# Conversion of the second layer's output weights begun at the end of the attention at a lower pace, and the seven-product block's sums taken from copies over three pairs

## The chip, the core and the metric

The kernel runs on one core of a Trainium2 chip. The engines that matter are TensorE (PE, with its weight loads PEld), VectorE (DVE), ScalarE (ACT) and the queue on which SyncE (SP) issues transfers. The metric is device microseconds of one execution; lower is better.

## The reference

Everything is float32. Attention for 4 batches, 8 heads, 576 positions and 64 columns per head, half of the heads with a local and half with a strided causal mask; its output, as a matrix x of 2304 tokens by 512, goes through two feed-forward layers of the same shape:

```python
h = np.maximum(x @ w_in, 0.0)       # 512 -> 2048
x = (h * h) @ w_out                 # 2048 -> 512, twice, with weights of their own
```

## The kernel before

**Precision.** The matrix engine takes each float32 operand as two parts, a high one (a ScalarE copy into `F32R`) and the rest (VectorE's difference). A product is three matmuls: high by high, high by rest, rest by high. So every operand costs one ScalarE copy and one VectorE subtraction.

**First layer.** Tokens go in blocks k = 0 to 4 of 512, except block 3 of 256. A step s is one slice of 128 hidden units (two slices in a block of 256). The loop runs `mm1(s + 1)` (24 matmuls of 256 columns, or 12 of 512), then `mm2(s)` (as many), and between groups of matmuls it calls `point()`, 8 times a step, where other work is put into the program. Blocks 0 to 2 are steps 0 to 47, block 3 is 48 to 55, block 4 is 56 to 71. `mm1` ends with ScalarE making `r`, `sq`, `gh` and VectorE making `gl`; `mm2` of that step needs `gh` first and `gl` last. At a block's end ScalarE copies four banks to `o` (tag `pt`, two buffers), and each `o` is stored to `y_dram`.

**Attention** fills points up to step 46 or 47.

**Conversion of the second layer's weights** (`conv2`). Its 32 pieces arrive as 64-bit words and are put together by shifts on VectorE and a scaling on ScalarE (`sign2`, `range2`, `whole2`), split (`high2`, `rest2`), and combined into four sums (`sums_1`, `sums_2`, `high_s`, `sums_3`). Pieces go in pairs, first 8 pairs of w_out, then 8 of w_in, 9 rows of the list `conv2` to a pair; a point adds `PACE` to a credit, and each whole credit puts one row into the program. A pair of w_out writes 1 MB of units into the first half of a staging area in `xall` (stored by L378 to `w_mem`) and 1 MB of sums into the second half (stored by L427). The area is single: `high2` of the next pair waits for the store by L378, `high_s` of the next for the store by L427. ScalarE runs in program order, so `r`, `sq` and `gh` of a step stand behind these copies.

**Second layer.** Block 5 (256 tokens; steps 72 to 79) is done by `narrow`, which reads units back (`narrow_w`, `ring_load`) and prepares the operands of the next block (`x_works`, `load_x`). Its last step and the four blocks after it use a scheme of seven products (`seven`, `frame`): per pair q of hidden slices one frame of 84 matmuls of 256 columns. A frame has four visits, which make hidden values in one bank `ps_m`: (11, s2), then (12), then (s1, s3), then (s4, 22); between them, as gaps of 9, 9, 15 and 9 matmuls, the products of the pair before, into seven banks. A visit writes over `ps_m`, so it waits for the additions by VectorE (L1080) that read the visit before. At a block's end the seven banks are summed (`first_sum`, `sums_late`, `sums_then`) and stored, while the next block's products begin to write over them. During a block the operands of the next are made from its `y_dram`, one of `x_works` per frame.

Of the kernel before, what the change touches and what calls it, by code (L numbers as in the profile page):

```python
# [17 lines left out]
P = 128  # L18
# [44 lines left out]
PACE, START_2 = 0.72, 4  # L63
# [106 lines left out]
def tile_attention_then_two_mlps(  # L170
# [263 lines left out]
    for i in range(0, half2 + 2, 2):  # L434
        old, new = i > 0, i < half2
        if new:
            conv2 += [[(sign2, i)], [(sign2, i + 1), (range2, i)]]
        conv2.append([(sums_3, i - 2)] * old + [(range2, i + 1)] * new)
        if new:
            conv2 += [  # L440
                [(whole2, i)],
# [583 lines left out]
    def mm2(s, point):  # L1025
# [28 lines left out]
        for m, (i, c, y, lhsT, rhs) in enumerate(todo):  # L1054
# [19 lines left out]

    def parts(hi, lo, src):
        nc.scalar.activation(out=hi, in_=src, func=AF.Copy)  # L1076
        tt(lo, src, r32(hi), ALU.subtract)
# [45 lines left out]

    def narrow(s, point):
# [4 lines left out]
        if q + 1 < NF // 2:  # L1129
            if q == 0:  # L1130
                load_x(NB + 1)
            else:
                for one in work[q - 1]:
                    one()
# [9 lines left out]
        for one in work[-1]:  # L1144
            one()
        todo = narrow_products(s)
        frame([todo[3 * i:3 * i + 3] for i in range(4)], (NB + 1, 0), None)
# [20 lines left out]
    def load_x(k):  # L1168
        t0, n = BLOCKS[1][k - NB]
        for c in range(KC):  # L1170
            nc.sync.dma_start(out=others[:, c * TB:(c + 1) * TB], in_=y_dram[:, c, t0:t0 + n])

    def x_works(k):
# [5 lines left out]
        def nothing():  # L1179
            pass  # L1180

        def op(i, src):
            return lambda: parts(*x_op(k, i), src)

        return [
            (nothing, op(0, b11)),
            (nothing, op(2, b21)),
            (lambda: tt(b11, b12, b11, ALU.subtract), op(3, b11)),
            (lambda: tt(b12, b22, b12, ALU.subtract), op(4, b12)),
            (lambda: tt(b11, b22, b11, ALU.subtract), op(1, b11)),  # L1190
            (lambda: tt(b21, b21, b11, ALU.subtract), nothing),
            (op(5, b22), op(6, b21)),
# [25 lines left out]
    def g_op(name):  # L1218
        tile, i = {
            "11": ("b", 0), "a22t4": ("b", 1), "s2t2": ("b", 2), "s4b22": ("b", 3),  # L1220
            "s1t1": ("a", 0), "s3t3": ("a", 1), "12": ("a", 2),
# [54 lines left out]
    def frame(gaps, nxt, cur, heads=(), copy=None, early=None, work=None, late=()):  # L1276

        k, q = nxt
        if not of:
# [6 lines left out]
            of["al"] = gpool.tile([P, 3 * HALF], F32R, tag="gl", name="al", bufs=2).rearrange(  # L1286
                "p (i n) -> p i n", i=3)
# [3 lines left out]
        heads = list(heads)  # L1291
        s24 = None
        if cur:
# [5 lines left out]
            nc.scalar.activation(out=ah[:, 2], in_=a12, func=AF.Copy)  # L1299
            if heads:  # L1300
                for one in heads[:2]:
                    one()
                tt(al[:, 2], a12, r32(ah[:, 2]), ALU.subtract)
                for one in heads[2:]:
                    one()
            tt(s13[:, 0], a21, a22, ALU.add)
            tt(s13[:, 1], a11, a21, ALU.subtract)
            if not heads:
                tt(al[:, 2], a12, r32(ah[:, 2]), ALU.subtract)
# [6 lines left out]
        u2, u3 = m[:, HT:], u[:, HT:]  # L1316
        u4 = u[:, :HT]
        nc.scalar.activation(out=m, in_=ps, func=AF.Copy, scale=W_BACK)  # L1318
        if cur:
            nc.scalar.activation(out=ah[:, 0:2], in_=s13, func=AF.Copy)  # L1320
            nc.scalar.activation(out=bh[:, 2:4], in_=s24, func=AF.Copy)
        tt(u2, m[:, :HT], m[:, HT:], ALU.add)
# [270 lines left out]
```

## Time and profile before

| what | value |
|---|---|
| median of 3 runs | 945.41 us (944.93 to 946.8) |
| the profiled execution | 947.56 us, of which the span from first to last instruction is 945.8 us |
| PE busy | 881.1 us, 93% |
| DVE busy | 685.6 us, 72% |
| ACT busy | 521.2 us, 55% |
| DMA | 155.21 MB, mean 164 GB/s |
| mean granted TensorE clock | 0.98 |

PE is busy nearly all the time, so what counts is where its stages take longer than their matmuls do. In time order: start and attention beside blocks 0 to 2 to about 364 us, blocks 3 and 4 to about 536, block 5 to about 589, the frames of seven products to 926, the last products and sums to 945.8.

### The profile page before, as it was taken

What the parts mean: (1) busy time and instruction counts of PE and PEld (TensorE: products, weight loads), DVE (VectorE), ACT (ScalarE), POOL (GpSimd) and SP (SyncE); (2) the same over time, 40 slices, a digit from 0 to 9 for tenths busy, and PEclk for the clock granted to TensorE, in tenths of its full rate; (3) what the DMA queues carried; (4) which work ended last, traced back from release to release, by engine and by line L of the source; (5) the groups of instructions that cost most, each with busy time, mean ns of one, the idle gap of its engine ahead of it and who ended that gap; (6) DMA issues with size and microseconds to landing.
All of it is one profiled execution on the core that took longest, in us unless ns stands there. A gap on an engine that the chain in (4) does not pass through costs nothing.

```text
span 945.8 us, 16062 instructions
## 1 busy us (share of the span) xinstructions
PE 881.1 (93%) x5719; PEld 784.4 (83%) x5719; DVE 685.6 (72%) x1745; ACT 521.2 (55%) x1201; POOL 17.7 (2%) x15
## 2 busy tenths in 40 slices
PE   8899999999999999979788779999989989998998
PEld 8788888888888889957566668999989989998998
DVE  5898973887767752766568766677877786777766
ACT  6887773676666553555456644544434444444442
POOL 0700000000000000000000000000000000000000
PEclk9999999999999999988989989999999999999999
DMA  8955512222221203487773285555575566555563
GB/s 271 342 181 169 188 42 75 66 84 73 87 92 59 61 11 116 154 298 286 265 256 100 85 295 195 178 168 169 184 227 172 178 202 209 170 172 185 187 189 124
DMA packets 81247, 155.21 MB, mean 164 GB/s; under 512 B 7440, under 2 KB 36240, under 8 KB 78096
## 3 DMA queue, kind: packets, MB, share of 16 engines
q1 hardware_dynamic: 81168, 154.19, 49.3%
q8 instruction: 45, 0.74, 0.3%
q14 instruction: 34, 0.28, 0.1%
HBM read 127.95 MB, written 26.21 MB: 163 GB/s over the span
## 4 chain that ended last, share of the span: by engine, by line
PE 58%; DVE 21%; ACT 11%; DMA 7%; issue 3%; SPq 0%; DVEq 0%; ACTq 0%
PE ps_h L969 15%; PE ps_y L969 14%; PE ps_m L1237 13%; PE ps_y L1264 7%; DMA w_mem<-xall 3%; DVE s L386 3%; DVE r L1080 2%; DVE bl L386 2%; PE ps_s L626 2%; DVE xall L386 2%; PE ps_x L702 2%; DVE gl L1022 2%; PE ps_pt L758 1%; ACT sq L1017 1%; ACT gh L1018 1%
## 5 line engine op out<-in xcount | busy, mean ns | idle before, releaser
L969 PE MATMUL ps_h<-xall,w 128*128 128x512 f32 (+1 forms) x1153 | 247.4, 358 | 0.0
L969 PEld LDWEIGHTS ps_h<-xall,w 128*128 128x128 f32 x1153 | 185.5, 189 | 26.2
L969 PE MATMUL ps_y<-gh,w 128*128 128x512 f32 (+1 forms) x640 | 162.8, 386 | 25.3 <-ACT gh L1018 18.8
L969 PEld LDWEIGHTS ps_y<-gh,w 128*128 128x128 f32 x640 | 109.7, 193 | 48.9 <-ACT gh L1018 24.5
L1237 PE MATMUL ps_m<-xall,s 128*128 128x256 f32 x768 | 113.5, 292 | 18.0 <-DVE r L1080 9.5
L1237 PEld LDWEIGHTS ps_m<-xall,s 128*128 128x128 f32 x768 | 99.3, 194 | 28.4 <-DVE r L1080 17.7
L1022 DVE TENSOR_TENSOR gl<-sq,gh 128x512 fp32r<-128x512 f32 x80 | 55.3, 691 | 61.8 <-ACT gh L1018 55.5
L1264 PE MATMUL ps_y<-w,bh 128*128 128x256 f32 x496 | 93.5, 281 | 0.0
L969 PE MATMUL ps_y<-gl,w 128*128 128x512 f32 (+1 forms) x324 | 85.8, 377 | 0.0
L1012 ACT ACTIVATE r<-ps_h 128x512 f32<-128x512 f32 x80 | 47.4, 592 | 65.8 <-PE ps_h L969 56.9
L1237 PE MATMUL ps_m<-xall,w 128*128 128x256 f32 x576 | 82.7, 279 | 0.0
L1264 PEld LDWEIGHTS ps_y<-w,bh 128*128 128x128 f32 x496 | 76.7, 190 | 0.0
L1237 PEld LDWEIGHTS ps_m<-xall,w 128*128 128x128 f32 x576 | 74.0, 188 | 0.4 <-ACT u L1318 0.4
L386 DVE TENSOR_TENSOR bl<-r,bh 128x256 fp32r<-128x256 f32 x64 | 27.2, 425 | 64.8 <-ACT bh L1076 37.1
L1264 PE MATMUL ps_y<-w,ah 128*128 128x256 f32 x372 | 70.9, 279 | 0.0
L1021 DVE TENSOR_TENSOR sq<-r 128x512 f32<-128x512 f32 x41 | 28.3, 691 | 58.2 <-ACT r L1012 58.2
L1264 PE MATMUL ps_y<-w,bl 128*128 128x256 f32 x248 | 69.4, 280 | 0.0
L969 PEld LDWEIGHTS ps_y<-gl,w 128*128 128x128 f32 x324 | 56.9, 192 | 10.8 <-DVE gl L1022 1.0
L1264 PEld LDWEIGHTS ps_y<-w,ah 128*128 128x128 f32 x372 | 57.0, 189 | 0.0
L1264 PE MATMUL ps_y<-w,al 128*128 128x256 f32 x186 | 52.6, 283 | 0.0
L674 ACT ACTIVATE s<-s,m 96x128 f32<-96x128 f32 (+2 forms) x88 | 34.3, 390 | 33.1 <-DVE m L558 32.5
L1299 ACT ACTIVATE ah<-c 128x256 fp32r<-128x256 f32 x31 | 13.0, 418 | 69.0 <-DVE c L1246 68.8
(121 smaller groups left out, 1510.5 us busy)
## 6 DMA issues: line engine op xcount, KB each, us to landing
w<-w_mem SPq DMA_DIRECT2D x221, 256.0 KB, 2.7
raw<-moe_w_in_d SPq DMA_DIRECT2D x32, 512.0 KB, 6.1
w_mem<-xall SPq DMA_DIRECT2D x16, 1024.0 KB, 5.2
raw<-moe_w_out_d SPq DMA_DIRECT2D x24, 512.0 KB, 5.0
xall<-w_mem SPq DMA_DIRECT2D x8, 1024.0 KB, 5.4
qk<-loc_qk_d SPq DMA_DIRECT2D x12, 416.0 KB, 3.0
out_d<-o SPq DMA_DIRECT2D x17, 256.0 KB, 3.9
y_dram<-o SPq DMA_DIRECT2D x16, 256.0 KB, 2.0
```

The lines of the kernel that those rows point to most:

```text
L386: nc.vector.tensor_tensor(out=out, in0=in0, in1=in1, op=op)
L626: nc.tensor.matmul(sv[:, h, g], lhsT=t[:, (h * ng + g) * nq:(h * ng + g + 1) * nq], rhs=t[:, 2 * ng * nq + g * ks:2 * ng * nq + g * ks + n ...
L674: nc.scalar.activation(out=blk, in_=blk, func=AF.Exp, scale=-1.0, bias=m[:nq, j:j + 1], accum_out=dens[i][:nq, j:j + 1],)
L702: nc.tensor.matmul(ps[:, 2 * g * nq:2 * (g + 1) * nq], lhsT=v[:nk, g * P:(g + 1) * P], rhs=pt[:, :, g], start=True, stop=True,)
L969: nc.tensor.matmul(y[:, c:c + w], lhsT=lhsT, rhs=rhs[:, c:c + w], start=start and c == 0, stop=stop and c + w == n,)
L1012: nc.scalar.activation(out=r, in_=ps, func=AF.Relu, scale=W_BACK)
L1021: nc.vector.tensor_tensor(out=sq, in0=r, in1=r, op=ALU.mult)
L1022: nc.vector.tensor_tensor(out=lo, in0=sq, in1=r32(h), op=ALU.subtract)
L1080: nc.vector.scalar_tensor_tensor(out=dst, in0=src, scalar=sign * W_BACK, in1=to, op0=ALU.mult, op1=ALU.add)
L1237: nc.tensor.matmul(ps[:, half * HT:(half + 1) * HT], lhsT=w[:, j * P:(j + 1) * P], rhs=x[:, j], start=half == 0 and j == 0 and m == 0, sto ...
L1264: nc.tensor.matmul(banks[name][:, t * HALF:(t + 1) * HALF], lhsT=g[:, rows], rhs=w, start=first and t == 0 and m == 0, stop=end and t == 1 ...
L1299: nc.scalar.activation(out=ah[:, 2], in_=a12, func=AF.Copy)
```

## The change

The conversion. It begins when the attention's last row has been put into the program, not at step 50; its first four loads are issued there too; the pace is 0.6 rows a point for w_out's pairs and 0.68 for w_in's, in place of 0.72. `sums_3` becomes a row of its own, and its store goes ahead of the load that used to precede it. The stores of `y_dram` of blocks 3 and 4 are issued by ScalarE.

The frames. VectorE's first addition after visit (12) goes ahead of the two subtractions (`al`, `bl` of 512 columns) that stood before it; the additions after visit (s1, s3) go ahead of the subtraction of `bh[0]` and of the next block's operand. Each of the next block's operands is subtracted for in the frame after the one that makes its sum. At a block's end ScalarE copies four banks into `others`, where VectorE's sums read them, spread over pairs 0, 1 and 2 of the next block; the next block's input is loaded into the same memory in two halves, after pairs 1 and 2.

```diff
-PACE, START_2 = 0.72, 4
+PACES = 0.6, 0.68
@@ sums_3
         if i < NF:
-            load2("out")
             nc.sync.dma_start(
                 out=w_mem[i // 2][:, 4 * U:8 * U],
                 in_=r32(xall[:, units_at + 4 * U:units_at + 8 * U]),
             )
+            load2("out")
@@ conv2
-        conv2.append([(sums_3, i - 2)] * old + [(range2, i + 1)] * new)
...
+        if i:
+            conv2.append([(sums_3, i - 2)])
+        if i < half2:
             conv2 += [
-                [(whole2, i)],
+                [(sign2, i)],
+                [(sign2, i + 1), (range2, i)],
+                [(whole2, i), (range2, i + 1)],
@@ mm2
-                nc.sync.dma_start(out=y_dram[:, c, t0:t0 + n], in_=t)
+                queue = nc.scalar if j >= NB - 2 else nc.sync
+                queue.dma_start(out=y_dram[:, c, t0:t0 + n], in_=t)
@@ x_works
+        def work(sums, *ops):
+            return (
+                sums,
+                [lambda i=i, t=t: high(x_op(k, i)[0], t) for i, t in ops],
+                [lambda i=i, t=t: rest(*x_op(k, i), t) for i, t in ops],
+            )
...
-            (lambda: tt(b11, b12, b11, ALU.subtract), op(3, b11)),
+            work(sub(b11, b12, b11), (2, b21)),
+            work(sub(b12, b22, b12), (3, b11)),
@@ frame
+        each(copies[0])
         ps = ps_h.tile([P, TB], F32, tag="h", name="ps_m")
         visit(k, q, ps, ("11", 0), ("s2", 1))
...
         nc.scalar.activation(out=m, in_=ps, func=AF.Copy, scale=W_BACK)
+        tt(u2, c11, u2, ALU.add)
+        each(copies[1])
         if cur:
-            tt(al[:, 0:2], s13, r32(ah[:, 0:2]), ALU.subtract)
-            tt(bl[:, 2:4], s24, r32(bh[:, 2:4]), ALU.subtract)
...
+            high(ah[:, 0:2], s13)
+            high(bh[:, 2:4], s24)
+        each(copies[2])
...
         visit(k, q, ps, ("12", 2))
-        add(a11, ps[:, :HT], m[:, :HT])
+        add(c11, ps[:, :HT], c11)
         if cur:
+            rest(bh[:, 2:4], bl[:, 2:4], s24)
+            rest(ah[:, 0:2], al, s13)
+        each(sums_x)
...
+        positive(a11, c11)
+        high(bh[:, 0], a11)
...
         add(u3, ps[:, HT:], u2)
         add(a22, ps[:, :HT], u3)
         add(u4, ps[:, :HT], u2)
...
+        rest(bh[:, 0], bl[:, 0], a11)
+        if not end:
+            each(rest_x)
@@ sums_then
+        def copy(name):
+            return lambda: nc.scalar.activation(
+                out=kept[name], in_=old[name], func=AF.Copy, scale=W_BACK)
...
+        copies = [copy("12")], [copy("a22t4"), copy("s1t1")], [copy("s3t3")]
+        return copies, [
+            ([lambda: tt(o12, kept["s1t1"], u, ALU.add)], [c12]),
+            ([c11], [lambda: tt(u, u, kept["s3t3"], ALU.add), c22]),
+            ([c21], []),
+        ]
@@ seven
+            if more and q in (1, 2):
+                load_x(k + 1, q - 1)
@@ the program's loop, in point()
-                elif (k, f) >= (NB - 2, START_2):
-                    credit[0] += PACE
+                elif n_att[0] >= att_end[-1] and n_conv2[0] < len(conv2):
+                    if not n_load2["out"]:
+                        for _ in range(4):
+                            load2("out")
+                    credit[0] += PACES[conv2[n_conv2[0]][0][1] >= NF]
```

On SP's queue, at the pairs of w_out around the end of block 3, the rows before are these (L378 stores units, L427 stores sums, L225 loads pieces, L1068 stores the block's result):

```order
L378 DMA w_mem_92<-xall 128x2048
L225 DMA raw<-moe_w_out_d 128x1024
L427 DMA w_mem_92<-xall 128x2048
L225 DMA others<-moe_w_out_d 128x1024
L1068 DMA y_dram<-o 128x256 x4
L378 DMA w_mem_93<-xall 128x2048
```

And after the change, at the same pairs (L426 is the store of the sums now):

```order
L378 DMA w_mem_92<-xall 128x2048
L426 DMA w_mem_92<-xall 128x2048
L225 DMA raw<-moe_w_out_d 128x1024
L225 DMA others<-moe_w_out_d 128x1024
L378 DMA w_mem_93<-xall 128x2048
```

The two stores of a pair now follow each other, the loads stand behind them, and the four stores of the block's result have left this queue. At the end of block 4 the queue held, before:

```order
L1092 DMA xall<-w_mem_90 128x2048
L1068 DMA y_dram<-o 128x512 x4
L225 DMA raw<-moe_w_in_d 128x4x256
L1213 DMA w<-w_mem_90 128x512
L1092 DMA xall<-w_mem_91 128x2048
```

And now:

```order
L1103 DMA xall<-w_mem_90 128x2048
L225 DMA raw<-moe_w_in_d 128x4x256
L1230 DMA w<-w_mem_90 128x512
L1103 DMA xall<-w_mem_91 128x2048
```

The second read of units (`narrow_w(1)`, the last row) no longer stands behind stores that wait for block 4's results. On DVE, the rows of one frame that makes no operand of the next block, from the sum `u2` on (the first row), were before:

```order
L386 TENSOR_TENSOR u<-u 128x256
L386 TENSOR_TENSOR al<-s,ah 128x512
L386 TENSOR_TENSOR bl<-s,bh 128x512
L1080 SCALAR_TENSOR_TENSOR r<-ps_m,u 128x256
L386 TENSOR_TENSOR bl<-r,bh 128x256
L1080 SCALAR_TENSOR_TENSOR u<-ps_m,u 128x256
L1080 SCALAR_TENSOR_TENSOR r<-ps_m,u 128x256
```

And are now:

```order
L386 TENSOR_TENSOR u<-u 128x256
L1091 SCALAR_TENSOR_TENSOR u<-ps_m,u 128x256
L386 TENSOR_TENSOR bl<-s,bh 128x512
L386 TENSOR_TENSOR al<-s,ah 128x512
L1091 SCALAR_TENSOR_TENSOR u<-ps_m,u 128x256
L1091 SCALAR_TENSOR_TENSOR r<-ps_m,u 128x256
```

The addition that reads visit (12) (the first row `<-ps_m,u`) moved ahead of the two wide subtractions, and the subtraction `bl<-r,bh` has gone from between it and the additions that read visit (s1, s3).

## Rows read from the trace of the kernel before

**Rows 1.** Windows: us; busy of PE, PEld, DVE, ACT, POOL; granted clock, DMA share, GB/s.

```profile
402.00:441.40 39.40, 31.50 (x160) 25.72 (x159) 25.54 (x47) 21.09 (x35) 0.00 (x0) 0.87 0.73 269
441.40:491.20 49.80, 38.26 (x146) 29.44 (x145) 31.04 (x56) 24.82 (x40) 0.00 (x0) 0.90 0.80 286
491.20:536.50 45.30, 40.19 (x183) 31.66 (x182) 37.19 (x68) 28.67 (x47) 0.00 (x0) 1.00 0.34 113
640.34:651.01 10.67, 10.30 (x87) 9.89 (x85) 8.34 (x19) 5.08 (x11) 0.00 (x0) 1.00 0.56 174
671.76:683.13 11.37, 10.24 (x86) 9.86 (x85) 9.54 (x21) 6.09 (x13) 0.00 (x0) 1.00 0.52 163
683.13:697.18 14.05, 11.70 (x86) 11.49 (x85) 10.12 (x22) 4.78 (x10) 0.00 (x0) 0.88 0.83 271
905.49:915.61 10.12, 10.08 (x87) 9.88 (x86) 7.12 (x17) 4.56 (x10) 0.00 (x0) 1.00 0.58 175
```

**Rows 2.** Timeline of PE, steps 48 to 79: start, duration, operation, count, [idle before].

```profile
363.81 2.90 PE L969 MATMUL ps_h<-xall,w 128*128 128x256 f32 x24
...
401.95 2.88 PE L969 MATMUL ps_h<-xall,w 128*128 128x256 f32 x24
...
415.31 2.90 PE L969 MATMUL ps_h<-xall,w 128*128 128x512 f32 x12
...
441.36 2.88 PE L969 MATMUL ps_h<-xall,w 128*128 128x512 f32 x12
...
491.18 2.88 PE L969 MATMUL ps_h<-xall,w 128*128 128x512 f32 x12
...
536.53 2.90 PE L969 MATMUL ps_h<-xall,w 128*128 128x256 f32 x24
...
553.87 3.61 PE L1113 MATMUL ps_y<-xall,gh 128*128 128x512 f32 x8 [6.54 <-DMA xall<-w_mem]
...
588.81 0.87 PE L1237 MATMUL ps_m<-xall,w 128*128 128x256 f32 x6
```

**Rows 3.** Timeline of ACT, three waits for transfers in that stretch.

```profile
370.70 1.26 ACT L1067 ACTIVATE o<-ps_y 128x512 f32<-128x512 f32 x2 [1.66 <-DMA y_dram<-o]
...
402.60 1.06 ACT L420 ACTIVATE xall<-others 128x1024 fp32r<-128x1024 f32 x1 [3.53 <-DMA w_mem<-xall]
...
426.07 0.71 ACT L1067 ACTIVATE o<-ps_y 128x256 f32<-128x256 f32 x2 [4.01 <-DMA y_dram<-o]
```

**Rows 4.** Timeline of SP's queue: stores of staged units and sums, and block 4's end.

```profile
392.47 0.33 SPq L378 DMA_DIRECT2D w_mem<-xall  x1
...
396.08 0.43 SPq L427 DMA_DIRECT2D w_mem<-xall  x1
...
481.50 0.32 SPq L378 DMA_DIRECT2D w_mem<-xall  x1
...
541.52 3.75 SPq L1068 DMA_DIRECT2D y_dram<-o  x4
...
546.43 0.42 SPq L1092 DMA_DIRECT2D xall<-w_mem  x1
```

**Rows 5.** Timeline of PE in the frames: first frame, two waits, last frame.

```profile
597.77 0.87 PE L1237 MATMUL ps_m<-xall,w 128*128 128x256 f32 x6
...
648.47 0.97 PE L1237 MATMUL ps_m<-xall,s 128*128 128x256 f32 x6 [0.28 <-DVE u L1080]
...
689.93 2.64 PE L1237 MATMUL ps_m<-xall,s 128*128 128x256 f32 x12 [2.35 <-DVE r L1080]
...
925.74 0.87 PE L1237 MATMUL ps_m<-xall,w 128*128 128x256 f32 x6
```

**Rows 6.** Timeline of DVE in two of those frames.

```profile
643.68 0.68 DVE L386 TENSOR_TENSOR bl<-s,bh 128x512 fp32r<-128x512 f32 x1
644.28 0.41 DVE L1080 SCALAR_TENSOR_TENSOR r<-ps_m,u 128x256 f32<-128x256 f32 x1
...
683.60 1.28 DVE L1080 SCALAR_TENSOR_TENSOR o<-ps_y,o 128x512 f32<-128x512 f32 x2
```

More of the change, by code (lines that the diff above doesn't have):

```diff
@@ L1122, in narrow_products, with all_of @@
         return [lambda m=m, t=t: one(m, *t) for m, t in enumerate(todo)]
+    def all_of(work):
+        for part in work:
+            each(part)
     def narrow(s, point):
@@ L1130, in narrow @@
             if q == 0:
[L1131 to L1134, printed above, removed]
+                load_x(NB + 1, 0)
+                load_x(NB + 1, 1)
+            elif q > 1:
+                all_of(work[q - 2])
             mm1(s + 1, point)
@@ L1143, in narrow @@
             conv2_by(1)
-        for one in work[-1]:
-            one()
+        all_of(work[-1])
         todo = narrow_products(s)
-        frame([todo[3 * i:3 * i + 3] for i in range(4)], (NB + 1, 0), None)
+        frame([todo[3 * i:3 * i + 3] for i in range(4)], (NB + 1, 0), False)
         t0, n = BLOCKS[1][0]
@@ L1274, in n_unit, with frame @@
         return [lambda t=t: half(t) for t in range(2)]
-    def frame(gaps, nxt, cur, heads=(), copy=None, early=None, work=None, late=()):
+    def frame(gaps, nxt, cur, copies=((), (), ()), end=False, x=((), (), ()), late=()):
         k, q = nxt
@@ L1348, in frame @@
         add(u4, ps[:, :HT], u2)
-        nc.scalar.activation(out=a22, in_=a22, func=AF.Relu)
-        nc.scalar.activation(out=a22, in_=a22, func=AF.Square)
-        nc.scalar.activation(out=bh[:, 1], in_=a22, func=AF.Copy)
-        for one in gaps[2]:
-            one()
-        for one in late:
-            one()
-        tt(bl[:, 1], a22, r32(bh[:, 1]), ALU.subtract)
+        positive(a22, a22)
+        high(bh[:, 1], a22)
+        rest(bh[:, 0], bl[:, 0], a11)
+        if not end:
+            each(rest_x)
+        each(gaps[2])
+        each(late)
+        rest(bh[:, 1], bl[:, 1], a22)
         visit(k, q, ps, ("s4", 5), ("22", 6))
@@ L1359, in frame @@
         squares(of["c"])
-        for one in gaps[3]:
-            one()
+        each(gaps[3])
     def first_sum():
@@ L1453, in seven @@
     def seven():
-        heads, tail = (), None
+        copies, sums = None, []
         for n, (k, q) in enumerate(pairs7[:-1]):
@@ L1459, in seven @@
             more = k < last7
+            x = [[], [], []]
             if more and q == 0:
[L1461 removed]
                 x_work[k + 1] = x_works(k + 1)
[L1463 to L1475 removed]
+            if more and q > 1:
+                x = [list(part) for part in x_work[k + 1][q - 2]]
+            late = [lambda: sums_late(not more)] if end else []
+            if sums:
+                first, then = sums.pop(0)
+                x[0] += first
+                late += then
+            frame(gaps, pairs7[n + 1], True, copies or ((), (), ()), end, x, late)
+            copies = None
+            if more and q in (1, 2):
+                load_x(k + 1, q - 1)
             if end and more:
[L1477 removed]
+                copies, sums = sums_then(k)
         finish()
@@ L1539, in point @@
                         credit[0] -= 1.0
-            if (k, f) == (NB - 2, 0):
-                for _ in range(4):
-                    load2("out")
             if k == NB:
```

142 lines of the change are left out of this document (60 added, 82 removed).

## The prediction, as made before the result was known

> **What bounds the kernel now.** I read the page first: PE is busy 93% of the span, so a gain can only come from stretches in which PE's own work takes longer than its matmuls. I then read PE's timeline for the starts of equal pieces of work. In the first layer a step is the same amount of work everywhere. From 363.81 to 401.95 us lie seven steps [rows 2], so an undisturbed step takes 38.14 / 7 = 5.45 us. From there to 588.81 lie 25 more, which would take 136.2 us and take 186.9: 50.6 us are lost. By stretch [rows 2], always the length less 5.45 us a step:
>
> - 401.95 to 415.31, two steps: 2.5 us
> - 415.31 to 441.36, three steps, in the first of which block 3's result is copied out: 9.7
> - 441.36 to 491.18, six steps, w_out's pairs beside the loads of w_in: 17.1
> - 491.18 to 536.53, seven steps, w_in's pairs: 7.2
> - 536.53 to 588.81, seven steps, block 4's end and block 5: 14.1
>
> The waits say why. ScalarE stands still for 3.53 us before `high_s` until a store of the staging area has landed, and for 4.01 us before block 3's `o` until an earlier `o` has [rows 3]; `r`, `sq` and `gh` queue behind it, and PE waits for `gh`. The windows add that the granted clock averages 0.87 and 0.90 there and 1.00 at 491 to 536 [rows 1]: after a long wait of PE part of the stretch runs at 1.2 instead of 2.4 GHz. At 553.87 PE waits 6.54 us for a read of units [rows 2] whose issue, at 546.43, stood on SP's queue behind block 4's four stores of 541.52 [rows 4].
>
> The frames are a second place. From 597.77 to 925.74 there are 30 [rows 5], 327.97 us. A step is 48 matmuls of 256 columns, so one takes 5.45 / 48 = 0.1135 us, and a frame's 84 take 9.54 us; 30 would take 286. I listed the 30 starts: 16 frames that make an operand of the next block take about 10.7 us, 8 plain ones 10.1, three that end a block 11.4, three that follow a block's end 14.0 (one of each kind in [rows 1]). They lose 42 us. The rest (the start up to 364 us, the frame before 597.77, the tail after 925.74) keeps its order.
>
> **The conversion, term by term.** One row of `conv2` is worth 1 / pace points, and a step has 8 points. A pair of w_out has 9 rows: 12.5 points, 1.56 steps or 8.5 us before; 15 points, 1.875 steps or 10.2 us now. In the trace the eight pairs did not keep 8.5: L378 is issued at 392.47 and, seven pairs later, at 481.50 [rows 4], 12.7 us each. The cycle through the single staging area explains it. From `high2` to the store are 4 rows, 5.6 points, 3.8 us; a store takes up to 6.5 us from its issue at 396.08 [rows 4] to the ScalarE copy that it releases at 402.60 [rows 3] (I take 5 to 6.5): 8.8 to 10.3 us, more than the 8.5 that the pace allows, and the issues that stand behind other rows of the queue add the rest. Now `high_s` stands 7 rows behind its store (7.9 us) and `high2` 5 rows (5.7 us), so the waits shrink to 0 to 1 us, which ScalarE has free in a step: `gh` is needed 5.45 us after `mm1` ends and takes three operations. Bytes per pair are two stores of 1 MB and two loads of 0.5 MB, 3.15 MB, 308 GB/s at 10.2 us; the windows show 269 and 286 GB/s at a DMA share of 0.73 and 0.80 [rows 1], so full share is about 360. From block 4 on each step adds a load of 0.5 MB (96 GB/s): 404 wanted, too much. The earlier start is what keeps this overlap as short as it is: 8 pairs of 1.875 steps from step 46.5 end at step 61.5, against 62.5 before. So of w_out's stretches I keep 1 us (0 to 3) of the first 2.5, and 6 (1 to 13) of the 17.1.
>
> VectorE must also follow. At 491 to 536 it is busy 37.19 us over seven steps [rows 1], 5.3 of each 5.45. Taking 0.69 off for `gl` leaves 4.6 a step, 7.2 a pair; at 0.68 rows a point (1.65 steps a pair) it needs 7.2 / 1.65 + 0.69 = 5.05, 93% in place of 97. I keep 3.5 (1 to 7) of 7.2: less crowded, not idle.
>
> Block ends. Block 2's end now falls into the first pair. Its third `o` already waited 1.66 us for a store with nothing else on the queues [rows 3]; with loads beside it I add 1 us (0 to 3). Block 3's stores leave SP's queue, so stores of units no longer stand behind them; the third `o` still waits for the first to land: 3 (0 to 7) stay of 9.7. An issue on ScalarE has no row here; an issue takes about 0.4 us of SP's queue [rows 4], so four cost ScalarE 0 to 1.6 us per block, inside these bounds. In the last stretch the read of 546.43 can be issued when `mm1` of block 5's first step is done, some 5 us earlier, and the 6.54 us wait and its clock loss go; each operand of `narrow` is made from a sum finished a step earlier. I keep 4 (1 to 8) of 14.1.
>
> Kept: 1 + 6 + 3.5 + 1 + 3 + 4 = 18.5 us (3 to 41) of 50.6, **a gain of 32 us** (10 to 48).
>
> A rule of the Trainium skill speaks against the block-end term. "DMA: Bandwidth & Descriptors", section "Issuing engines are not separate DMA queues", says that transfers issued from another engine run on the same 16 DMA engines and only save the sequencer's issue time. By it eight moved stores would be worth about 3 us. The trace bears out that the engines are shared, but the 6.54 us wait comes from the order of issues on one queue, not from bandwidth. The rival below has its price.
>
> **The frames, term by term.** Two waits in a frame of 10.67 us. First, `r<-ps_m,u`, which reads visit (12), starts at 644.28 behind `bl` of 643.68 [rows 6] and `al` before it; put ahead of both it starts when visit (12) is done, at about 643.5, and the 0.3 us that PE waits before (s1, s3) go. Second, the next block's sum, `bl<-r,bh` and the next operand's rest stand between it and the additions after (s1, s3); (s4, 22) starts at 648.47 [rows 5], 8.13 us into a frame of which 63 matmuls take 7.15; with these moved behind, some 0.5 us go. VectorE is not the limit: 8.34 us busy in such a frame, 7.12 in a plain one [rows 1]. So 9.85 and 9.7.
>
> After a block's end VectorE runs four sums out of the banks before its own work, 0.64 us each [rows 6], and PE waits 2.35 us, at a clock that then falls (the 12 matmuls take 2.64 us, [rows 5]; 0.88 mean, [rows 1]). Now ScalarE's copies free the banks: 0.63 us each by the same kind of copy in [rows 3], four make 2.5 us on an engine that is busy 4.78 of this frame [rows 1]. VectorE has two sums in pair 0 (7.12 + 1.3 = 8.4 us), three in pair 1 (9.1), one in pair 2. So 10.1 for pairs 0 and 1. The frame that ends a block makes two rests and one sum: 7.12 + 2.1 = 9.2 against 9.54 measured; 10.2. The next block's input now lands only in pairs 2 and 3; the copy that needs it stands mid-frame, 5 us in, behind loads issued at the frame's start.
>
> Sum of 30: 15 frames with an operand at 9.85, three ends at 10.2, six of pairs 0 and 1 after an end at 10.1, six others at 9.7: 147.8 + 30.6 + 60.6 + 58.2 = 297.2, **a gain of 31 us** (12 if only the first wait goes and the block ends halve; 42 at 9.54 each).
>
> **Sum.** 947.56, the profiled execution's own time (span 945.8), less 32 and 31 is 884.6. That execution lies 2.15 us above the median of 945.41, so on the runs' scale 882.5: **883 us**.
>
> **The rivals.**
> - *The staging area still sets the pace* (12.7 us a pair as measured): 8 × (12.7 − 10.2) = 20 us lost in place of 7: 896. For it: the same single area, and 404 GB/s wanted from block 4 on. Against it: a slower pace and stores first.
> - *VectorE and ScalarE keep the frames* near the upper end: copies and operand hold back ScalarE's squares, and only 12 of 31 us come: 902. Against it: both are under 9.6 us busy in every kind.
> - *Moved stores bring only issue time* (the skill's rule above, as order on a queue that doesn't matter): 6.7 of block 3's end and 6.5 of the last stretch stay: 896.
> - *Slower than before.* The pairs of w_out slow each other down: if loads and stores together make a pair take 18.9 us or more, 8 × (18.9 − 10.2) less the 7 already counted eats all 63 us. The seven gaps between L378 average 12.7 beside a faster pace, so it needs a cost that no row shows.
> - *No change*: the order of rows changes but every wait finds another partner, 944. The fixed 9.54 us of a frame and the 7.12 us of VectorE leave no reason for it.
>
> **How the numbers follow.** Forecast 0.54, staging area 0.17, frames 0.12, stores 0.09, several of these together 0.05 (about 912), no change 0.01, slower 0.02. For 8 in 10 I take 866 (frames at 9.6, conversion near its lower bounds) to 910, which holds the three single rivals; the forecast's own range is 868 to 898. Faster by over 0.2% (about what a measurement of this kernel can tell from no change) 0.97, within 0.2% 0.01, slower 0.02.
>
> **What the profile will show.** Right: 25 steps from the end of the seven undisturbed ones that lose under 20 us; ScalarE's waits for `w_mem` under 1.5 us and rarer up to block 4; clock near 1.00; no wait for units in block 5; frames of 9.6 to 10.2 us with no 14; PE's wait for DVE `r` gone. Wrong: `high_s` or `high2` still waiting 3 us for stores, a pair of L378 further apart than 11 us, a wait of ScalarE for `others`, or frames of 10.5. The forecast falls if the stores, not the order of issue, were what ScalarE waited for.

## The result, and the profile after

The changed kernel takes 893.74 us (median of 4 runs, 893.21 to 894.45) against 945.7 before: a ratio of 0.945 (95% interval 0.9434 to 0.9467), 52 us faster. Forecast were 883 us, with a range of 866 to 910. The profiled execution has a span of 892.2 us, 53.6 less than before. The page:

```profile
span 892.2 us, 16045 instructions
...
PE 858.4 (96%) x5719; PEld 772.6 (87%) x5719; DVE 684.3 (77%) x1742; ACT 528.5 (59%) x1216; POOL 17.7 (2%) x15
```

The windows of the stretch in which the weights are converted, of nine, five, five, six and seven steps in turn (block 3's end opens the second), and then of one frame and of the 30 frames; columns as in [rows 1]:

```profile
363.80:414.60 50.80, 49.87 (x414) 48.59 (x413) 39.52 (x74) 32.69 (x52) 0.00 (x0) 1.00 0.74 269
414.60:449.30 34.70, 30.73 (x122) 23.71 (x121) 21.30 (x38) 18.36 (x30) 0.00 (x0) 0.90 0.77 276
449.30:482.60 33.30, 28.18 (x122) 22.31 (x122) 24.78 (x46) 20.07 (x32) 0.00 (x0) 1.00 0.67 214
482.60:525.30 42.70, 34.88 (x159) 27.18 (x158) 31.42 (x58) 24.58 (x40) 0.00 (x0) 1.00 0.42 141
525.30:570.60 45.30, 41.41 (x261) 36.75 (x260) 30.24 (x50) 24.57 (x40) 0.00 (x0) 0.96 0.64 218
...
579.52:589.24 9.72, 9.72 (x86) 9.72 (x85) 7.45 (x18) 5.49 (x12) 0.00 (x0) 1.00 0.59 191
579.52:872.21 292.69, 292.68 (x2523) 292.00 (x2521) 246.65 (x536) 156.59 (x338) 0.00 (x0) 1.00 0.67 211
```

The 30 frames take 292.69 us where [rows 5] gave 327.97: 35.3 us gained, 31 forecast. PE is busy for all of it. Nearly every frame lasts 9.72 us; those that end a block 9.89 to 9.96, those after an end 9.79 to 9.86.

The conversion gained less. From 364.03 us to the first visit at 570.70 lie the same 32 steps as from 363.81 to 588.81 in [rows 2]; at 5.45 us each they would take 174.4, and they take 206.7. So 32.3 us are still lost of 50.6: 18.3 gained, 32 forecast. With the prediction's numbers of steps to a stage (nine up to 414.59, three up to 438.36, six up to 474.88, seven up to 525.31, seven more; length less 5.45 us a step) the losses are 1.5, 7.4, 3.8, 12.3 and 7.3. The stages do not follow the pairs exactly: w_out's last pair is stored at 456.89 (units) and 460.50 (sums), so of the 3.8 only 1.7 stand beside w_out's pairs, and the nine steps behind them, up to 525.31, lose 14.4 beside w_in's. 35.3 and 18.3 are the 53.6 of the span.

Two places say why. The first is block 3's end, on PE and on ACT:

```profile
414.59 2.90 PE L969 MATMUL ps_h<-xall,w 128*128 128x512 f32 x12
418.24 1.54 PE L969 MATMUL ps_y<-gh,w 128*128 128x512 f32 x4 [0.74 <-ACT o L1067]
421.27 1.22 PE L969 MATMUL ps_y<-gh,w 128*128 128x512 f32 x2 [1.49 <-ACT o L1067]
424.15 1.22 PE L969 MATMUL ps_y<-gh,w 128*128 128x512 f32 x2 [1.66 <-ACT o L1067]
```

```profile
415.04 1.06 ACT L420 ACTIVATE xall<-raw 128x1024 fp32r<-128x1024 f32 x1 [1.13 <-DMA w_mem<-xall]
...
418.21 0.35 ACTq L1069 DMA_DIRECT2D y_dram<-o  x1
...
420.83 0.38 ACT L1067 ACTIVATE o<-ps_y 128x256 f32<-128x256 f32 x1 [1.84 <-DMA y_dram<-o]
421.25 0.33 ACTq L1069 DMA_DIRECT2D y_dram<-o  x1
423.71 0.38 ACT L1067 ACTIVATE o<-ps_y 128x256 f32<-128x256 f32 x1 [2.50 <-DMA y_dram<-o]
```

The wait for the staging area is down from 3.53 us in [rows 3] to 1.13, as forecast. But the third and fourth `o` each wait for the store of the `o` two before them, because tag `pt` has two buffers, and PE waits for the `o`s to free its banks.

The second place is the stretch of w_in's pairs. One step of it on DVE, ACT and PE:

```profile
497.22 0.69 DVE L268 SCALAR_TENSOR_TENSOR val<-raw 128x512 int32<-128x512 int32 x1
497.94 0.76 DVE L386 TENSOR_TENSOR s<-val 128x256 f32<-128x256 f32 x2
500.48 0.69 DVE L1022 TENSOR_TENSOR gl<-sq,gh 128x512 fp32r<-128x512 f32 x1 [1.77 <-ACT gh L1018]
501.08 0.42 DVE L386 TENSOR_TENSOR s<-s,val 128x256 f32<-128x256 f32 x1
```

```profile
494.79 0.69 ACT L263 ACTIVATE raw<-raw 128x512 f32<-128x512 f32 x1 [1.83 <-DVE raw L246]
...
498.00 0.63 ACT L368 ACTIVATE w<-val 128x512 fp32r<-128x512 f32 x1 [0.63 <-DVE val L268]
...
499.81 0.63 ACT L1018 ACTIVATE gh<-sq 128x512 fp32r<-128x512 f32 x1
502.00 1.06 ACT L420 ACTIVATE s<-s 128x1024 fp32r<-128x1024 f32 x1 [1.56 <-DVE s L386]
```

```profile
495.91 2.88 PE L969 MATMUL ps_h<-xall,w 128*128 128x512 f32 x12
500.50 2.14 PE L969 MATMUL ps_y<-gh,w 128*128 128x512 f32 x8 [1.70 <-ACT gh L1018]
```

All three wait, and none is full: in 42.70 us DVE is busy 31.42 and ACT 24.58, the clock is 1.00, the DMA share 0.42. DVE stands 1.77 us at `gl`, which needs `gh`. `gh` stands on ACT behind a row of the conversion that waited for DVE's `val`. DVE's next sums stand behind `gl`, and ACT then waits 1.56 us for those. Each engine keeps its order, and each order holds up the other: a ring, in which the rows behind one `gl` on DVE hold up ACT, and the next `gh`, behind its rows on ACT, holds up the next `gl`. From the `gl` at 493.00 to the one at 500.48 are 7.48 us, and the step of PE from 495.91 to 503.39 takes 7.48 as well. This is the theory tested below.

### The profile page after: what moved, and what is told of

Its sections match the earlier page's. It is cut to its first block, busy times and chain, and to the rows that moved or that the text cites. A ratio compares the mean times of both kernels' runs of the same rounds, so it can differ in the third digit from the quotient of the medians.

```text
span 892.2 us, 16045 instructions
## 1 busy us (share of the span) xinstructions
PE 858.4 (96%) x5719; PEld 772.6 (87%) x5719; DVE 684.3 (77%) x1742; ACT 528.5 (59%) x1216; POOL 17.7 (2%) x15
## 5 line engine op out<-in xcount | busy, mean ns | idle before, releaser
L969 PE MATMUL ps_y<-gh,w 128*128 128x512 f32 (+1 forms) x640 | 159.7, 379 | 18.5 <-ACT gh L1018 13.6
L969 PEld LDWEIGHTS ps_y<-gh,w 128*128 128x128 f32 x640 | 107.5, 189 | 40.9 <-ACT gh L1018 17.8
L1256 PE MATMUL ps_m<-xall,s 128*128 128x256 f32 x768 | 104.8, 279 | 0.6 <-DVE u L1091 0.6
L1256 PEld LDWEIGHTS ps_m<-xall,s 128*128 128x128 f32 x768 | 95.5, 188 | 1.8 <-DVE u L1091 1.1
L1021 DVE TENSOR_TENSOR sq<-r 128x512 f32<-128x512 f32 x38 | 26.3, 691 | 48.8 <-ACT r L1012 48.8
L1091 DVE SCALAR_TENSOR_TENSOR u<-ps_m,u 128x256 f32<-128x256 f32 x96 | 40.5, 421 | 26.4 <-PE ps_m L1256 26.2
L1081 ACT ACTIVATE ah<-c 128x256 fp32r<-128x256 f32 x33 | 13.7, 417 | 71.8 <-DVE c L1265 71.7
L263 ACT ACTIVATE raw<-raw 128x512 f32<-128x512 f32 x49 | 33.1, 676 | 32.8 <-DVE raw L246 32.4
```

The costliest lines, as they stand in the source:

```text
L263: nc.scalar.activation(out=upper, in_=upper, func=AF.Copy, scale=2.0 ** (W_EXP // 8 - 112))
L969: nc.tensor.matmul(y[:, c:c + w], lhsT=lhsT, rhs=rhs[:, c:c + w], start=start and c == 0, stop=stop and c + w == n,)
L1021: nc.vector.tensor_tensor(out=sq, in0=r, in1=r, op=ALU.mult)
L1091: nc.vector.scalar_tensor_tensor(out=dst, in0=src, scalar=sign * W_BACK, in1=to, op0=ALU.mult, op1=ALU.add)
L1256: nc.tensor.matmul(ps[:, half * HT:(half + 1) * HT], lhsT=w[:, j * P:(j + 1) * P], rhs=x[:, j], start=half == 0 and j == 0 and m == 0, sto ...
```

## The experiments

The table gives each median, its runs, the ratio to the kernel before with its 95% interval, and the median less 893.74. The kernel before measured 945.4, 947.29 and 946.93 us beside the first four, second four and last four kernels, so differences between kernels are good to some 2 us.

| kernel | us | ratio | less 893.74 |
|---|---|---|---|
| e1_frames_only | 909.71 (909.44 to 911.03) | 0.9621 [0.9601, 0.9641] | +16.0 |
| e2_conversion_only | 928.72 (926.6 to 929.95) | 0.9824 [0.98, 0.9848] | +35.0 |
| e3_stores_on_sp | 896.17 (895.88 to 897.01) | 0.9477 [0.9458, 0.9496] | +2.4 |
| e4_four_o | 890.36 (890.16 to 891.41) | 0.9416 [0.9397, 0.9435] | -3.4 |
| e5_late_gl | 876.64 (875.9 to 878.21) | 0.9259 [0.9244, 0.9275] | -17.1 |
| e6_old_start | 905.89 (903.71 to 906.32) | 0.9558 [0.9542, 0.9574] | +12.2 |
| e7_old_pace | 898.25 (896.52 to 901.49) | 0.9489 [0.9467, 0.9511] | +4.5 |
| e8_rests_ahead | 907.84 (907.33 to 909.44) | 0.959 [0.9574, 0.9605] | +14.1 |
| e9_rests_between | 909.29 (907.52 to 910.73) | 0.9599 [0.9581, 0.9618] | +15.6 |
| e10_no_copies | 901.21 (901.03 to 901.98) | 0.9521 [0.9503, 0.9538] | +7.5 |
| e11_late_gl_four_o | 865.39 (864.49 to 866.12) | 0.914 [0.9123, 0.9157] | -28.4 |
| e12_old_rows | 901.21 (899.35 to 902.41) | 0.9517 [0.9498, 0.9537] | +7.5 |

### The two halves apart: e1_frames_only and e2_conversion_only

The first is the changed kernel with `sums_3`, `conv2`, the stores of y, paces and start of before:

```diff
-PACES = 0.6, 0.68
+PACE, START_2 = 0.72, 4
...
-                elif n_att[0] >= att_end[-1] and n_conv2[0] < len(conv2):
...
-                    credit[0] += PACES[conv2[n_conv2[0]][0][1] >= NF]
+                elif (k, f) >= (NB - 2, START_2):
+                    credit[0] += PACE
```

> The changed kernel with its conversion of w_out's and w_in's units as in the kernel before (pace 0.72 from step 50, loads at step 48, the old order of rows, stores of blocks 3 and 4 on SP); only the frames of the second pass are the new ones. The prediction's terms give it -31 us, so about 914 us. The two traces, in which the 30 frames went from 327.97 to 292.69 us, give -35, so about 910 us. If the frames had gained only because the steps ahead of them ended otherwise, it would stay near 930 us. In its trace the frames should last 9.7 to 9.9 us each.

The second is the kernel before with these same lines in their changed form.

> The kernel before with only the conversion of w_out's and w_in's units changed (start with the end of the attention, paces 0.6 and 0.68, loads with the start, new order of rows, stores of blocks 3 and 4 on ScalarE's queue); the frames are the old ones. The prediction's terms give it -32 us, so about 913 us. The two traces (some 32 us still lost over the steps, of 50.6 before) give -18.5, so about 927 us. If the two parts help each other, this and the run with the frames alone would together give less than the 52 us of the whole change.

Measured 909.71 and 928.72 us: 35.7 and 16.7 below the 945.4 of before beside them. The 30 frames of the first take as long as in the changed kernel:

```profile
595.47:888.38 292.91, 292.90 (x2522) 292.16 (x2521) 246.54 (x536) 156.44 (x338) 0.00 (x0) 1.00 0.67 211
```

The halves add up to 52.4 of 52.0 us: no effect of one on the other shows within 2 us, the frames are worth a little more than forecast, and the shortfall is all in the conversion.

### The queue of y's stores: e3_stores_on_sp

```diff
-                queue = nc.scalar if j >= NB - 2 else nc.sync
-                queue.dma_start(out=y_dram[:, c, t0:t0 + n], in_=t)
+                nc.sync.dma_start(out=y_dram[:, c, t0:t0 + n], in_=t)
```

> The changed kernel with blocks 3's and 4's stores of y back on SP's queue. Theory A (order on a queue: on SP the stores stand behind loads that wait for room in the ring, and the third o of a block waits for the first store): slower by 6 to 13 us, with PE waits for ACT's o of 3 to 4 us at block 3's end, as before. Theory B (only who spends the issue time matters: eight issues of some 0.35 us go from ScalarE to SP): within 3 us of the changed kernel, and rather faster, 891 to 894 us.

2.4 us slower, little more than the 2 us to which differences are good: theory B's size, on the other side of the changed kernel. At block 3's end the queue makes no difference; its two `o`s wait 4.95 us together (4.34 in the changed kernel), and the first step of that end takes 12.36 us (12.28). At block 4's end the wait of [rows 2] is back:

```profile
420.70 0.38 ACT L1067 ACTIVATE o<-ps_y 128x256 f32<-128x256 f32 x1 [2.56 <-DMA y_dram<-o]
...
423.47 0.38 ACT L1067 ACTIVATE o<-ps_y 128x256 f32<-128x256 f32 x1 [2.39 <-DMA y_dram<-o]
```

```profile
539.99 3.75 PE L1123 MATMUL ps_y<-xall,gh 128*128 128x512 f32 x8 [6.38 <-DMA xall<-w_mem]
```

That step takes 14.63 us in place of 9.09, 5.5 more. But the three behind it take 5.58, 5.55 and 5.53 where the changed kernel takes 6.01, 7.55 and 5.53: while PE waits for the read, the other engines get on with the conversion, and about 3 us remain, less 0.8 that this trace was ahead by then. So order on the queue does make a wait, as the prediction said, and its price is only what is not caught up. By the rule of the Trainium skill that the prediction weighed ("DMA: Bandwidth & Descriptors", section "Issuing engines are not separate DMA queues") the moved stores were to be worth an estimated 3 us. The measured sum agrees with it; the 6.38 us wait says that more than issue time is at work.

### Buffers for the output: e4_four_o

```diff
-                t = apool.tile([P, 512], F32, tag="pt", name="o")[:, :n]
+                t = apool.tile([P, 512], F32, tag="s" if j >= NB - 2 and c > 1 else "pt", name="o")[:, :n]
```

> The changed kernel with the third and fourth o of blocks 3 and 4 in another tag (tag s, whose tiles are free by then), so that no o waits for the store of one before it. Theory A (the 1.84 and 2.50 us that the third and fourth o wait for a store at block 3's end are what PE waits for there, 3.9 us in three waits, and the lower clock after it is their consequence): 4 to 7 us faster, 887 to 890 us. Theory B (the rows of the conversion ahead of the o's on ScalarE keep them, so that PE waits as long for something else): within 1 us of 893.7.

3.4 us faster, theory A at a little less than its size. At block 3's end the four `o`s now run without a wait for a store, the step takes 7.41 us, and the clock no longer falls (1.00 where the changed kernel has 0.90):

```profile
418.56 0.38 ACT L1067 ACTIVATE o<-ps_y 128x256 f32<-128x256 f32 x1 [0.40 <-ACT o L1067]
419.35 0.39 ACT L1067 ACTIVATE o<-ps_y 128x256 f32<-128x256 f32 x1 [0.40 <-ACT o L1067]
```

```profile
414.60:449.30 34.70, 31.37 (x130) 23.44 (x128) 22.86 (x40) 20.73 (x35) 0.00 (x0) 1.00 0.83 294
```

Of the 4.9 us that the step gains, some 2 go again in waits for `gh` in the next steps (3.4 us between 410 and 455, 1.3 in the changed kernel). Block 4's end gains 1.6 us (7.49 in place of 9.09) and the step behind it loses 1.5 again. So buffers remove block 3's wait and the other queue does not. They are not the only thing that does: e5, below, leaves `o` with two buffers and takes the same step in 6.87 us.

### The ring of orders: e5_late_gl

```diff
+LATE_GL = 6
...
-        nc.vector.tensor_tensor(out=lo, in0=sq, in1=r32(h), op=ALU.subtract)
+        def rest_of_g():
+            nc.vector.tensor_tensor(out=lo, in0=sq, in1=r32(h), op=ALU.subtract)
+
+        if 0 < n_conv2[0] < len(conv2):
+            late_gl.append(rest_of_g)
+        else:
+            rest_of_g()
...
+                if n_pt[0] == LATE_GL:
+                    while late_gl:
+                        late_gl.pop(0)()
```

> The changed kernel with VectorE's subtraction for gl put six points later into its step while units are converted, so that it stands behind the conversion's rows of that step instead of ahead of them. Theory A (a ring of orders: in the stretch of w_in's pairs VectorE stands idle before gl until ScalarE has made gh, gh stands behind rows of the conversion on ScalarE, and these wait for rows that stand behind gl on VectorE; PE's waits for gh of 1.3 to 2.0 us, about one a step, are its price): the 10 us lost over w_in's pairs fall to 3 or less and block 5's with them, 5 to 10 us faster, 884 to 889 us. Theory B (the rows simply keep ScalarE and VectorE too busy for a step of 5.45 us): within 1.5 us of 893.7.

17.1 us faster, about twice the upper end of theory A, with no operation fewer. The edit holds `gl` until the sixth point of a step. In the program `gl` stood between the third and the fourth, so it now stands behind the rows of two points, 1.2 to 1.4 rows of the conversion, and not six points later as the expectation says. It acts on w_out's pairs too. Waits of PE from 363 us to the frames, in the changed kernel and then here (columns: sum, times, longest):

```profile
PE ps_y L969 <- ACT gh L1018: 12.9, 8, 2.0
PE ps_y L969 <- ACT o L1067: 4.8, 5, 1.7
PE ps_y L1124 <- ACT gh L1018: 3.6, 2, 1.8
```

```profile
PE ps_y L971 <- ACT gh L1020: 4.3, 6, 1.1
PE ps_y L1132 <- ACT gh L1020: 2.5, 1, 2.5
PE ps_y L971 <- ACT o L1075: 1.7, 3, 0.7
```

PE's waits for `gh` fall from 16.5 to 6.8 us, and DVE's at `gl` from 45.5 to 19.4 (363 to 590 us). By the stages above this kernel loses 1.5, 1.4, 0.9, 5.9 and 5.4 us. The seven w_in steps thus give 6.4 of 12.3, about half and not the fall to 3 that theory A forecast, and what keeps the 5.9 and 5.4 is not shown. Another 6.0 come from block 3's end, which theory A did not name: ScalarE reaches the first `o` there at 414.82 in place of 417.82, and though the third still waits 2.6 us for a store, PE waits only once:

```profile
419.04 1.57 PE L971 MATMUL ps_y<-gh,w 128*128 128x512 f32 x4 [0.74 <-ACT o L1075]
```

So the loss at block 3's end needs both, an `o` that waits for a store and a ScalarE that comes to it late; four buffers (e4) or the order (e5) takes most of it away. Theory B, that the rows are too many for a step, does not fit: DVE and ACT were under 75% busy in w_in's stretch, and half of the loss went with the place of one instruction. The Trainium skill ("Perfetto Trace Analysis", section "Tensor Engine Instruction (MATMUL, LD_WEIGHTS)") says that ScalarE and VectorE take their instructions strictly in order. The rows of the changed kernel above agree: the sums of the conversion that stand behind `gl` start at 501.08, after it, though `gl` waits 1.77 us.

### The start: e6_old_start

```diff
+START_2 = 4
...
-                elif n_att[0] >= att_end[-1] and n_conv2[0] < len(conv2):
-                    if not n_load2["out"]:
-                        for _ in range(4):
-                            load2("out")
+                elif (k, f) >= (NB - 2, START_2) and n_conv2[0] < len(conv2):
...
+            if (k, f) == (NB - 2, 0):
+                for _ in range(4):
+                    load2("out")
```

> The changed kernel with the old start: first row of the conversion at step 50, loads at step 48, paces 0.6 and 0.68 kept. Theory A (the start matters, since the conversion takes longer at these paces and must end before block 5 reads its units back): the conversion ends some three steps, 18 us, later, PE waits again for units in block 5, and it takes 5 to 15 us more, 899 to 909 us. Theory B (the start only shifts the same losses): within 2 us of 893.7.

12.2 us slower, as theory A has it, but by a nearer cause than a read of units: block 5's `mm1` waits for units of w_in that DVE is only just finishing, four times, 10.7 us in all; two of them:

```profile
557.15 0.62 PE L970 MATMUL ps_h<-xall,w 128*128 128x256 f32 x3 [2.83 <-DVE w L376]
560.77 4.42 PE L970 MATMUL ps_h<-xall,w 128*128 128x256 f32 x19 [3.00 <-DVE w L376]
```

The start pays because block 5 is a deadline. The crowding of the queues, the prediction's reason for it, does not show: from 414.6 to 482.6 us the DMA engines run at shares of 0.89 and 0.91, and PE is busy 32.03 of the first 34.70 us, block 3's end among them, and 32.60 of the last 33.30.

### The pace: e7_old_pace

```diff
-PACES = 0.6, 0.68
+PACES = 0.72, 0.72
```

> The changed kernel with the old pace of 0.72 rows a point for both matrices; start, order of rows and queues as changed. Theory A (at 12.5 points a pair of w_out is shorter than the cycle of the staging area, so ScalarE waits for stores again and PE for gh): 4 to 10 us slower, 898 to 904 us. Theory B (the new order of rows alone gives the stores their time): within 1.5 us of 893.7, or a little faster, since less of the conversion is left in block 5.

4.5 us slower, at the lower end of theory A. Only part of its mechanism shows: up to 480 us ACT waits twice for the staging area before `high_s`, 4.3 us (once, 1.1, in the changed kernel), while PE's waits for `gh` grow from 5.1 to 9.7. How much of these comes from the ring was not separated. In this trace (896.52 us, the fastest of its runs) the nine steps before block 3's end lose 12.7 us where the changed kernel loses 1.5, and later steps give much back: w_in's seven lose 5.1 in place of 12.3, the last seven 3.5 in place of 7.3. So the lower pace pays beside w_out; whether 0.68 for w_in costs something by itself was not tried.

### The order of rows: e12_old_rows

```diff
-            load2("out")
...
+            load2("out")
...
-        if i:
-            conv2.append([(sums_3, i - 2)])
...
+        if new:
+            conv2 += [[(sign2, i)], [(sign2, i + 1), (range2, i)]]
+        conv2.append([(sums_3, i - 2)] * old + [(range2, i + 1)] * new)
```

> The changed kernel with the old order of rows in the conversion (first two rows of a pair ahead of the sums of the pair before, load ahead of the store); start, paces and queues as changed. Theory A (the prediction's step: the new order gives a store 7 rows, 7.9 us, before its staging area is wanted, in place of 5): ScalarE waits for stores again, 4 to 10 us slower, 898 to 904 us. Theory B (the slower pace alone gives the stores their time): within 2 us of 893.7. Faster than 891 us would say that the new order makes the ring between ScalarE and VectorE.

7.5 us slower: theory A. ACT waits six times for the staging area before `high_s`, 21.0 us in all, as often and nearly as long as in the kernel before (columns: sum, times, longest; the kernel before, then this one, then this one's longest wait):

```profile
ACT xall L420 <- DMA w_mem<-xall: 21.9, 6, 5.0
```

```profile
ACT xall L420 <- DMA w_mem<-xall: 21.0, 6, 5.0
```

```profile
456.51 1.06 ACT L420 ACTIVATE xall<-raw 128x1024 fp32r<-128x1024 f32 x1 [5.01 <-DMA w_mem<-xall]
```

So the slower pace alone takes nothing off these waits. The new order of rows, with the loads behind the stores, takes off most of them even at the old pace (4.3 us in e7), and both together leave 1.1. Start, pace, queue and rows, each undone alone, cost 26.6 us together, more than the 16.7 that the whole half brings: they lean on one another.

### The frames' terms: e8_rests_ahead, e9_rests_between, e10_no_copies

The first puts two subtractions back ahead of the addition of visit (12), the second the other two back ahead of the additions of (s1, s3), the third makes the sums at a block's end from the banks, five in a row at the next frame's start:

```diff
@@ e8_rests_ahead
+        if cur:
+            rest(ah[:, 0:2], al, s13)
+            rest(bh[:, 2:4], bl[:, 2:4], s24)
         each(gaps[0])
...
-        if cur:
-            rest(bh[:, 2:4], bl[:, 2:4], s24)
-            rest(ah[:, 0:2], al, s13)
@@ e9_rests_between
         high(bh[:, 0], a11)
+        rest(bh[:, 0], bl[:, 0], a11)
         if not end:
             each(high_x)
+            each(rest_x)
...
-        rest(bh[:, 0], bl[:, 0], a11)
-        if not end:
-            each(rest_x)
@@ e10_no_copies
-        copies = [copy("12")], [copy("a22t4"), copy("s1t1")], [copy("s3t3")]
...
+        return ([direct], [], []), [([], [c12]), ([], []), ([], [])]
```

> The changed kernel with the two subtractions for al and for the second half of bl put back ahead of the addition of visit (12) in VectorE's order of a frame. Theory A (the prediction's first wait: they delay the operand of the visits (s1, s3), 0.3 us in each frame): 8 to 10 us slower, 902 to 904 us, with frames of about 10.0 us. Theory B (the gain of the frames comes from what stands between that addition and the next ones, and from the block ends): within 2 us of 893.7.

> The changed kernel with the subtractions for bl of the first quarter and of the next block's operand put back ahead of the additions after the visits (s1, s3) in VectorE's order of a frame. Theory A (the prediction's second wait, some 0.5 us in each frame with an operand: 15 such frames, somewhat less in the others): 6 to 14 us slower, 900 to 908 us. Theory B (VectorE has slack there, since it is busy only 8.4 of 9.72 us): within 2 us of 893.7.

> The changed kernel without ScalarE's four copies out of the banks after a block's end; VectorE makes the sums straight from the banks at the start of the next frame, as in the kernel before, with the changed order in the rest of the frame. Theory A (the prediction's third term: VectorE's sums ahead of its own work cost the first frame after an end 4 us, three times): 9 to 13 us slower, 903 to 907 us, first frames of 13 to 14 us. Theory B (the changed order alone would have taken the wait away): within 2 us of 893.7.

14.1, 15.6 and 7.5 us slower: each term is real, two larger than theory A's range and one smaller, and their sum of 37.2 us is near the 35.3 of the whole. In the first a plain frame takes 10.08 us, with DVE busy 7.06; 0.35 more than 9.72, near the 0.3 forecast, and the three frames after a block's end 11.04, with a wait of PE for DVE's `u` of 1.05:

```profile
589.81:599.89 10.08, 10.00 (x87) 9.79 (x85) 7.06 (x17) 4.56 (x10) 0.00 (x0) 1.00 0.59 184
...
660.51:671.55 11.04, 9.99 (x87) 9.79 (x85) 8.35 (x19) 6.51 (x14) 0.00 (x0) 1.00 0.58 184
```

In the second, DVE waits for ACT at the operand's subtraction, and PE for what stands behind it:

```profile
605.34 0.69 DVE L386 TENSOR_TENSOR xall<-others,xall 128x512 fp32r<-128x512 f32 x1 [0.59 <-ACT xall L1081]
605.95 0.42 DVE L1091 SCALAR_TENSOR_TENSOR u<-ps_m,u 128x256 f32<-128x256 f32 x1
606.40 0.42 DVE L1091 SCALAR_TENSOR_TENSOR r<-ps_m,u 128x256 f32<-128x256 f32 x1
```

```profile
607.21 0.95 PE L1256 MATMUL ps_m<-xall,s 128*128 128x256 f32 x6 [0.66 <-DVE u L1091]
```

DVE is busy 7.81 us of such a frame's 10.56: again order, not load. In the third the first frame after an end takes 12.51 to 12.61 us, PE waiting in two places:

```profile
660.01 0.48 PE L1283 MATMUL ps_y<-w,ah 128*128 128x256 f32 x2 [0.97 <-ACT ah L1081]
...
662.81 0.50 PE L1283 MATMUL ps_y<-w,bh 128*128 128x256 f32 x2 [1.16 <-DVE o L1091]
```

That is 2.7 us more than 9.8. The other 1.5 of the 14.05 in [rows 1] does not come back; what this kernel keeps of the change, the order of the rest of the frame above all, accounts for it.

### The winners together: e11_late_gl_four_o

The edit of e5 with `gl` held until the eighth point, and that of e4 with `NB - 3`, so that block 2 has four `o`s too.

> The changed kernel with the two winners together: gl's subtraction held back to the eighth point of a step (the sixth in the run with late gl alone, 876.6 us), and the third and fourth o of blocks 2, 3 and 4 in a tag of their own. If late gl and the four o's remove different waits: 872 to 875 us. If the o's waited for stores only because the steps ahead of them ran late: 876 to 878 us. If gl now comes too late for PE: above 878 us, with PE waits for gl.

865.39 us, 28.4 below the changed kernel and faster than any of the three expectations. The 32 steps now end at 542.00 us and lose 3.8, of which 3.4 in the last seven and 0.3 in w_in's seven; PE is busy without a break through w_out's pairs and half of w_in's:

```profile
414.60:449.30 34.70, 34.70 (x154) 28.30 (x153) 27.95 (x50) 23.01 (x38) 0.00 (x0) 1.00 0.93 341
449.30:482.60 33.30, 33.30 (x149) 27.57 (x148) 31.45 (x58) 24.27 (x39) 0.00 (x0) 1.00 0.51 155
```

DVE's waits at `gl` are down to 6.4 us. DVE is busy 94% of the second window and PE loses nothing there. How much of the 11.3 us beyond e5 belongs to the two later points and how much to the buffers was not separated; e4 alone was worth 3.4.

## Why the prediction was right, and where its sizes were wrong

- **The time and the sign** were right: 893.7 lies inside the range, 10.7 us above the forecast. The conversion gained 13.7 us less than forecast (18.3 for 32) and the frames 4.3 more; that the two partly cancel is luck.
- **Undisturbed step, 5.45 us**: right; undisturbed steps take 5.44 to 5.48 us after the change as well.
- **w_out's pairs and the staging area**: right. 1.5 us are lost before block 3's end (1 for the stretch and 1 for block 2's end forecast) and 3.8 in the six steps given to w_out beside w_in's loads (6 forecast). e12 shows the mechanism by undoing it. The rival in which the area still sets the pace did not come about. The reason given for what stays, 404 GB/s wanted of the DMA engines, does not show: with only the order changed 0.9 of the 3.8 is left (e5), and e11 carries 341 GB/s from 414.6 to 449.3 us and loses next to nothing up to 482.6.
- **"VectorE must also follow"** is the step that failed: 3.5 us (1 to 7) kept for w_in's seven steps, measured 12.3, more than the 7.2 before. The prediction asked whether DVE has the time for its rows in a step, and DVE was busy only 74% of the stretch; in e11 it is busy 94% of such a stretch and PE loses nothing. What counts is where `gl` stands between those rows: moved by about one, it gave back 6.4 us here and 17.1 over the whole conversion (e5).
- **Block 3's end**: 3 us (0 to 7) kept, measured 7.4 with the step behind it. The prediction named the third `o`'s wait for the first to land and then gave most of the gain to the queue. e3 and e4 show that the queue is worth nothing there and a third and fourth buffer 4.9 us of the step; the order of `gl` alone is worth 5.4 of it (e5), a path that the prediction did not have.
- **The last stretch**: 4 us (1 to 8) kept, measured 7.3. The 6.54 us wait for units went as forecast and comes back with the stores on SP (e3), but only 2.4 us of it are net. What stays of the 7.3 is mostly two waits for `gh`, 1.84 us at 536.15 and 1.76 at 551.17, and a slower PE behind the first (the clock averages 0.96 in the window).
- **The frames**: 31 us forecast, 35.3 measured. The split was nearly right: the first wait at 0.3 us (0.35 in e8), the second at 0.5 (frames of e9 mostly 0.4 to 1.0 longer). It was too careful at 9.85 and 10.1 us a frame: with orders that do not hold each other up a frame that makes an operand takes 9.72, like any other. Its remark against the second rival, that both engines are under 9.6 us busy in every kind of frame, overlooks the 10.12 us of DVE in the 14.05 of [rows 1]; it changed no term of the sum.
- **The rival "moved stores bring only issue time"** is right about the sum of the moved stores (2.4 us) and wrong about the wait, which was real. That its 896 lies nearer to 893.7 than the forecast is luck: it leaves w_in's stretch and the frames as forecast, and both came out otherwise. The trace before could not bear out that the DMA engines are shared, as the prediction has it, since SP issued every transfer of the program there. The trace after does: from 414 to 428 us the transfers that ScalarE issued took 11.4% of the 16 engines' time and those of SP 63.6%.
- **Its own signs** were mixed. Met: one wait of 1.13 us for the staging area, no wait for units in block 5, frames of 9.7 to 10.0 us. Missed: 32.3 us lost where it wanted under 20, and a clock of 0.90 around block 3's end. Of its signs of being wrong two came: three of the seven gaps between stores of units were over 11 us (12.66, 15.55 and 12.17; mean 11.6, forecast 10.2), and ScalarE waited six times for `others`, 2.9 us in all, which cost PE nothing. The long gaps are not the single area's doing, since ScalarE waited only 1.13 us for it; the steps themselves were long.

## What to carry to other kernels

Where several engines wait and none is full, write down what stands behind what on each in-order engine and look for a ring; moving one instruction behind the work that its producer is waiting for was worth more here (17.1 us) than the change of pace (4.5). Ask of each wait for a transfer whether another buffer, or an engine that comes earlier, removes it before moving the transfer to another queue. Price a wait by what is still lost some steps later, since the work of other engines catches up meanwhile.

## What the runs showed of the hardware

- A transfer issued by ScalarE took 0.33 to 0.35 us of its queue in the changed kernel (the rows ACTq above), against 0.32 to 0.43 for one on SP in [rows 4]. Where four stores followed each other without waits it was up to 0.60 (e4) and 0.84 (e11).
- After three waits of PE that sum to 3.9 us within a step, the granted clock of the stretch averages 0.90, so part of it ran at the 1.2 GHz level; where e4 takes these waits away it is 1.00.
- With the DMA engines at a share of 0.93 and 341 GB/s for 34.70 us, PE was busy without a break (e11).
